# Attention and two mixture layers on one core: another start-up order, with mask rows of two pairs written in place and unread products

## The chip, the cores and the metric

The kernel runs on one core of a Trainium2 chip. The metric is the device time of one execution in microseconds; each version is run several times, and the median counts. The profile shows one execution, taken by the hardware profiler. The engines are named as in the profile: PE (TensorE, matrix products), PEld (its weight loads), DVE (VectorE), ACT (ScalarE), POOL (GpSimd), SP (SyncE, which issues all DMAs here).

## What is computed

A masked attention over 2 batches of 8 heads, then a soft mixture of experts, then a dense layer pair. All that the change touches is in the attention:

```python
def _attn_ref(q, k, v, proj):          # q, k, v: 2 x 8 x 768 x 64; proj: 64 x 6
    scale = 1.0 / np.sqrt(D)
    q_bits = (np.einsum('bhsd,dk->bhsk', q, proj) > 0).astype(np.int64)
    k_bits = (np.einsum('bhsd,dk->bhsk', k, proj) > 0).astype(np.int64)
    powers = 2 ** np.arange(n_bits)
    q_bucket = np.sum(q_bits * powers, axis=-1)
    k_bucket = np.sum(k_bits * powers, axis=-1)
    mask = q_bucket[:, :, :, None] == k_bucket[:, :, None, :]
    scores = scale * np.matmul(q, k.transpose(0, 1, 3, 2))
    scores = np.where(mask, scores, -1000000000.0)
    scores = scores - np.max(scores, axis=-1, keepdims=True)
    attn = np.exp(scores)
    attn = attn / (np.sum(attn, axis=-1, keepdims=True) + 1e-09)
    return np.matmul(attn, v).astype(np.float32)

x = _moe_ref(x=x, **moe_kwargs)        # x: 1536 x 512
return _moe2_ref(x=x, **moe2_kwargs)   # h = x @ w_in; (h - tanh(h)) @ w_out
```

## The kernel before

The 16 heads are worked in 8 pairs of two heads (0 to 7). For each pair, q and k come in by DMA (`load_qk`, tiles `tq`, `tk`), PE transposes them into PSUM (`t_unit`), ACT and DVE copy the result to `xq` and `xk` (128 rows: 64 of each head). The operands of the scores are the tiles `QA` and `KA` (per head 128 rows: rows 0 to 63 the rounded q or k, rows 64 to 87 the mask rows, row 96 the row of maxima) and `QB` and `KB` (rounded parts and what the rounding left over, written by `lo` and by the copies of `dups`). `his` writes the first 64 rows of `QA` and `KA`.

The mask rows come from the sign bits of q and k times `proj`. For pair 0, `bits0` makes two products of 24 rows and 768 columns on PE, DVE compares them with zero (`bt0`), and `rows0` scales the bits and writes them straight into rows 64 to 87 of `QA` or `KA`, on ACT, DVE or POOL. For all other pairs `bits` makes four products of 384 columns that stand in four column groups of PE, one comparison, one scaling (`rt`), and eight DMAs copy the rows from `rt` into `QA` and `KA`.

`m_unit` makes the scores of 128 queries (PE, `pm`, two products over 96 rows) and DVE takes their maxima (`mx`, one reduction for each of 12 blocks of a pair). `m_fin` transposes the maxima, and makes from them a row `row` for row 96 of `QA` and flags `zrow` of queries without a partner; both are copied by DMA, the flags four times into `z`. `v_unit` and `v_unit2` make a mean of v that those queries get. `s_unit` makes the scores `pst` from `KA`, `QA`, `KB`, `QB` (four products), ACT takes the exponential, POOL adds the results up (`es`), and `av_unit` multiplies with v into `pav`.

In PSUM one pool hands out three buffers in turn to all of `pt`, `pb`, `pm`, `pc`, `pv`, `pst` and to `cl` of the conversion of `w_in` (`win_load`, `win_cvt`: one ACT and three DVE instructions for each of 16 pieces `raw` of 512 KB). An instruction that needs a buffer waits for the last reader of what stood there three requests earlier.

Nothing here is ordered by a scheduler: the list `START` is worked off once, then `STEP` for each pair (`LAST` for the last). A word is a unit and the pair that it works on (in `STEP` the pair is the current one plus the unit's role). Each engine executes its own instructions in this order, and so does SP with its DMAs; a DMA is issued when what it waits for is done, and those behind it wait. At most eight DMAs are in flight: each waits for the one eight places ahead. `warm` in `START` makes PE products over zeros that nobody reads.

Of the kernel before, what the change touches and what calls it, by code (L numbers as in the profile page):

```python
# [1337 lines left out]
```

## Time and profile before

| | us |
|---|---|
| median of 3 runs | 494.92 (493.47 to 500.78) |
| the profiled execution's own time | 497.41 |
| its span, first to last instruction | 495.5 |
| PE busy | 467.0 (94%) |
| DVE, POOL, ACT busy | 332.7, 298.6, 271.7 |
| mean granted PE clock | 0.963 of 2.4 GHz |

The span is what the views of the trace divide up; 1.9 us of the execution's own time lie around it. Busy times are sums over stages that have different limits, so a stage is read for itself, from its waits and from what each engine did in it. In the granted clock, 1.00 is 2.4 GHz and 0.50 is 1.2 GHz.

### The profile page before, as it was taken

How to read it: one execution, taken by the hardware profiler on the slowest of the kernel's cores; microseconds unless marked ns; L12 is line 12 of the kernel's file. 1: busy time of each engine (PE TensorE's matmuls, PEld its weight loads, DVE VectorE, ACT ScalarE, POOL GpSimd, SP SyncE). 2: the span in 40 equal slices, each digit the busy share in tenths (PEclk: the TensorE clock that was granted, in tenths of full speed). 3: DMA queues.
4: the chain of work that ended last, by engine and by line, in shares of the span. 5: the costliest groups of instructions: out<-in, count | busy, mean ns of one | idle time of the engine just before them, and what ended most of it. 6: DMA issues, size and time to landing. Idle time of an engine off the chain costs nothing.

```text
span 495.5 us, 7422 instructions
## 1 busy us (share of the span) xinstructions
PE 467.0 (94%) x2634; PEld 302.5 (61%) x2634; DVE 332.7 (67%) x493; ACT 271.7 (55%) x463; POOL 298.6 (60%) x243
## 2 busy tenths in 40 slices
PE   7869999999999999999999899998999999999995
PEld 3445555556556565665565534557767677888884
DVE  5948687787887968648323564669999997544451
ACT  6252846638466384653444111167888887766671
POOL 4866976779687797867953120015677775444431
PEclk9559999999999999999999899997999999999998
DMA  6518157191650906829598899995000002100003
GB/s 211 130 29 234 56 127 190 40 232 48 162 151 20 248 15 160 279 55 333 167 340 337 298 366 385 352 408 235 1 1 0 2 0 86 43 1 1 1 1 133
DMA packets 51572, 72.83 MB, mean 147 GB/s; under 512 B 25604, under 2 KB 33480, under 8 KB 51528
## 3 DMA queue, kind: packets, MB, share of 16 engines
q1 hardware_dynamic: 51528, 72.28, 46.1%
q8 instruction: 23, 0.38, 0.3%
q14 instruction: 21, 0.17, 0.1%
HBM read 60.08 MB, written 3.15 MB: 128 GB/s over the span
## 4 chain that ended last, share of the span: by engine, by line
PE 60%; DVE 17%; DMA 7%; ACT 6%; SPq 4%; POOL 2%; issue 2%; DVEq 0%; ACTq 0%; POOLq 0%
PE pav L523 9%; PE po L1228 6%; PE po L1229 6%; PE po L1230 6%; PE pst L496 5%; PE pm L445 5%; PE pst L498 4%; DVE win L186 4%; DMA QB<-QA 3%; DVE mx L446 2%; SPq L150 2%; DVE win L1179 2%; PE pt L352 2%; PE po L913 2%; DVE win L191 2%
## 5 line engine op out<-in xcount | busy, mean ns | idle before, releaser
L511 POOL TENSOR_TENSOR es<-es,e 128x768 f32<-128x768 f32 x59 | 118.6, 2022 | 23.5 <-ACT e L500 22.8
L500 ACT ACTIVATE e<-pst 128x768 f32<-128x768 f32 x96 | 76.6, 807 | 92.2 <-PE pst L498 88.5
L446 DVE TENSOR_REDUCE mx<-pm 128x1 f32<-128x768 f32 x96 | 88.0, 952 | 20.8 <-PE pm L445 19.9
L523 PE MATMUL pav<-e,tv 128*64 128x256 f32 (+1 forms) x384 | 72.9, 498 | 0.0
L1209 POOL TENSOR_TENSOR split<-win,split 128x512 fp32r<-128x512 f32 x31 | 44.0, 1420 | 45.6 <-ACT split L1204 45.5
L445 PE MATMUL pm<-KA,QA 96*128 96x512 f32 x192 | 55.6, 391 | 5.2 <-DMA QA<-rt 3.1
L1209 POOL TENSOR_TENSOR ghl<-win,ghl 128x256 fp32r<-128x256 f32 x32 | 27.6, 862 | 49.8 <-ACT ghl L1204 49.8
L496 PE MATMUL pst<-QA,KA 128*128 128x512 f32 x192 | 56.2, 374 | 1.3 <-DVE bt L364 1.3
L1178 DVE SCALAR_TENSOR_TENSOR ph<-win,ph 128x512 f32<-128x512 f32 x64 | 35.7, 558 | 29.8 <-ACT win L1173 29.8
L1228 PE MATMUL po<-w,split 128*128 128x512 f32 x128 | 51.5, 402 | 0.0
L1229 PE MATMUL po<-w,split 128*128 128x512 f32 x128 | 51.4, 401 | 0.0
L1230 PE MATMUL po<-w,split 128*128 128x512 f32 x128 | 51.2, 400 | 0.0
L498 PE MATMUL pst<-QB,KB 128*128 128x512 f32 x192 | 50.6, 345 | 0.0
L523 PEld LDWEIGHTS pav<-e,tv 128*64 128x64 f32 x384 | 24.0, 136 | 39.3 <-issue 39.1
L445 PEld LDWEIGHTS pm<-KA,QA 96*128 96x128 f32 x192 | 30.9, 201 | 27.3 <-issue 11.4
L505 POOL TENSOR_TENSOR es<-e 128x768 f32<-128x768 f32 x16 | 29.3, 1831 | 24.7 <-PE pr L534 17.7
L1173 ACT ACTIVATE win<-ph 128x512 f32<-128x512 f32 (+1 forms) x64 | 30.8, 482 | 24.0 <-PE ph L1166 23.9
L1179 DVE SCALAR_TENSOR_TENSOR win<-win,ph 128x512 f32<-128x512 f32 x64 | 35.5, 555 | 8.6 <-ACT win L1173 0.5
L1174 ACT ACTIVATE win<-win,ct 128x512 f32<-128x512 f32 (+1 forms) x64 | 39.5, 617 | 2.1
L496 PEld LDWEIGHTS pst<-QA,KA 128*128 128x128 f32 x192 | 29.9, 194 | 16.0 <-issue 8.1
L498 PEld LDWEIGHTS pst<-QB,KB 128*128 128x128 f32 x192 | 30.3, 194 | 4.4
L1230 PEld LDWEIGHTS po<-w,split 128*128 128x128 f32 x128 | 24.6, 192 | 5.7
(243 smaller groups left out, 814.6 us busy)
## 6 DMA issues: line engine op xcount, KB each, us to landing
w<-in_moe_w_dram SPq DMA_DIRECT2D x32, 1024.0 KB
raw<-in_moe_w_in_dram SPq DMA_DIRECT2D x16, 512.0 KB
w<-in_moe_w_out_dram SPq DMA_DIRECT2D x8, 1024.0 KB
tv<-in_v_dram SPq DMA_DIRECT2D x8, 384.0 KB
out_dram<-win SPq DMA_DIRECT2D x12, 256.0 KB
tq<-in_q_dram SPq DMA_DIRECT2D x14, 192.0 KB
tk<-in_k_dram SPq DMA_DIRECT2D x14, 192.0 KB
QB<-QA SPq DMA_DIRECT2D x10, 192.0 KB
```

The lines of the kernel that those rows point to most:

```text
L445: nc.tensor.matmul(pm[:, c0:c1], QA[s][h][:96, c * P:(c + 1) * P], KA[s][h][:96, c0:c1], start=True, stop=True)
L446: nc.vector.reduce_max(mx[i][:, h * KT + c:h * KT + c + 1], pm, axis=AX.X)
L496: nc.tensor.matmul(pst[:, c0:c1], KA[s][h][:, c * P:(c + 1) * P], QA[s][h][:, c0:c1], start=True, stop=False)
L498: nc.tensor.matmul(pst[:, c0:c1], KB[t][h][:, c * P:(c + 1) * P], QB[t][h][:, c0:c1], start=False, stop=True)
L500: nc.scalar.activation(e, pst, AF.Exp, scale=0.125)
L511: eng.tensor_tensor(es[i, h][0], es[i, h][0], e, ALU.add)
L523: nc.tensor.matmul(pav[i][j][64 * h:64 * h + 64, :], tv[i][:, h, c, :], e2[h][:, c0:c1], start=False, stop=c == KT - 1, tile_position=(0, ...
L1179: nc.vector.scalar_tensor_tensor(g, w, Q_B, self.ph[p], ALU.add, ALU.mult)
L1209: (eng or nc.gpsimd).tensor_tensor(gl[p], g, gh[p].bitcast(F32), ALU.subtract)
L1228: nc.tensor.matmul(po, gh[p][:, us], wo.half(f, 0), start=f == 0, stop=False)
L1229: nc.tensor.matmul(po, gh[p][:, us], wo.half(f, 1), start=False, stop=False)
L1230: nc.tensor.matmul(po, gl[p][:, us], wo.half(f, 0), start=False, stop=f == NF - 1)
```

## The change

`START` is another list. In it:

- q and k of pair 0 are asked for first, then the constants `ct`, then two pieces `raw` of `w_in`, and then `blk` and the four small loads of `proj`. q and k of pair 1 come before `phi` and v; v of pair 1 is loaded in `START` too.
- All mask rows of pair 0 are written by POOL, those of a head ahead of its first maximum (before: those of head 0 after its last maximum, so that its maxima were taken without them).
- `bits0` and `rows0` now serve any pair, and pair 1's mask rows are made by them and written in place by ACT (`KA`) and POOL (`QA`), ahead of pair 1's maxima; its eight DMAs from `rt` go.
- POOL instead of ACT copies three blocks of 64 rows (`hp1.0`, `hp0.0`, `hp3.1`).
- The four copies of the flags leave `m_fin` for a unit of their own, `m_flag` (`fz`), which stands later in `START` and right behind `f2` in `STEP`.
- A new unit `keep` makes unread products of 32 rows and 128 columns from `ct`, 26 of them in `START`, the last ahead of the first scores; `warm` makes four products instead of three, over `phiB` (zeros at that time), into a buffer of the pool of `pav`.
- A unit that was done already is left out when `STEP` comes to it. From the first scores on, the instructions stand in the same order on every engine, except SP's loads of `w_in` and v, which were partly issued before.

```diff
-START = ("const.0 warm.3 qk.0 const.1 tq_aaaa.0 wl.0 oi.0 tk_aavv.0 h1.0 h0.0 bq.0 wl.0 bk.0 h2.0 "
+START = ("qk.0 warm.4 const.0 wl.0 oi.0 wl.0 const.1 tq_aaaa.0 tk_aavv.0 keep.2 bq.0 hp1.0 hp0.0 h3.0 bk.0 wq0p.0 keep.2 "
...
         nc.vector.memset(ones32, 1.0)
-        nc.vector.memset(phiB, 0.0)
...
-        def bits0(which):
-            x = (xqs, xks)[which][0]
+        def bits0(i, which):
+            x = (xqs, xks)[which][i]
...
-        def rows0(which, h, eng):
+        def rows0(i, which, h, eng):
...
-                y, b = X[0][h][rs, c0:c1], bt0[which][:, c0:c1]
+                y, b = X[i][h][rs, c0:c1], bt0[which][:, c0:c1]
...
-            for r in range(4):
-                if r % 2 in hs:
-                    j = r % 2 - hs[0]
-                    copy(zr[i][r:r + 1], zrow[KT * j:KT * j + KT, :])
+            zrows.setdefault(i, []).append((hs, zrow))
+
+
+        def m_flag(i):
+            for hs, zrow in zrows.pop(i):
+                for r in range(4):
+                    if r % 2 in hs:
+                        j = r % 2 - hs[0]
+                        copy(zr[i][r:r + 1], zrow[KT * j:KT * j + KT, :])
...
+        done = set()
+
         def unit(w, i):
+            if w in ("m", "s0", "s1", "a", "wl", "wc", "lp", "warm", "keep", "const"):
+                if w == "m" and nm.get(i) == 2 * KT - 1:
+                    return
+            elif (w, i) in done:
+                return
...
-            elif w == "warm":
+            elif w in ("warm", "keep"):
+
+                w_ = 256 if w == "warm" else P
                 for _ in range(i):
-                    nc.tensor.matmul(wt[:32, :256], wz[:, :32], wz, start=True, stop=True)
+                    nc.tensor.matmul(wt[0][:32, :w_], wz[:, :32] if w == "warm" else ident[:, :32], wz if w == "warm" else ident, start=True, stop=True)
...
-        wt, wz = psum("warm"), e_p.tile([P, 256], F32, tag="e", name="warm")
+        wt, wz = [pav_p.tile([P, 512], F32, tag="pav512", name="warm")], phiB.rearrange("p a b c -> p (a b c)")
```

On SP at the start of the program there stood before (`x4` is four instructions in a row):

```order
L153 DMA ct<-in_const_dram 128x298
L316 DMA tq<-in_q_dram 128x2x384
L316 DMA tk<-in_k_dram 128x2x384
L157 DMA blk<-in_const_dram 4x128
L161 DMA projb<-in_proj_dram 64x6 x4
L617 DMA raw<-in_moe_w_in_dram 128x1024 x2
L167 DMA phiB<-in_moe_phi_dram 64x4x32 x2
L326 DMA tv<-in_v_dram 128x2x384
```

and there stands now, up to the same load of v:

```order
L316 DMA tq<-in_q_dram 128x2x384
L316 DMA tk<-in_k_dram 128x2x384
L154 DMA ct<-in_const_dram 128x298
L622 DMA raw<-in_moe_w_in_dram 128x1024 x2
L158 DMA blk<-in_const_dram 4x128
L162 DMA projb<-in_proj_dram 64x6 x4
L320 DMA tq<-in_q_dram 128x6x64 x2
L320 DMA tk<-in_k_dram 128x6x64 x2
L167 DMA phiB<-in_moe_phi_dram 64x4x32 x2
L151 DMA kh_264<-KA_131 64x768
L326 DMA tv<-in_v_dram 128x2x384
```

The constants moved behind q and k, two pieces of `w_in` moved from behind the four small loads of `proj` to ahead of them, and pair 1's q and k moved ahead of v.

On POOL, from the first clearing of `KA` on, there stood before:

```order
L295 MEMSET KA_131 64x1536
L299 MEMSET KA_131 1x1536
L395 ISA
L395 TENSOR_SCALAR QA_127<-bt_194,ct 24x768
L428 TENSOR_TENSOR KB_138<-xk,KA_131 64x768
L395 TENSOR_SCALAR QA_127<-bt_194,ct 24x768
L432 TENSOR_TENSOR KB_138<-xk,kh_254 64x768
```

and there stands now (`KA_131` and `QA_127` are the operands of pair 0; the row `ISA` carries no operands, and the trace has no record of it):

```order
L295 MEMSET KA_131 64x1536
L299 MEMSET KA_131 1x1536
L403 CAST QA_127<-xq 64x768
L403 CAST KA_131<-xk 64x768
L395 ISA
L395 TENSOR_SCALAR QA_127<-bt_195,ct 24x768
L395 TENSOR_SCALAR KA_131<-bt_204,ct 24x768
L428 TENSOR_TENSOR KB_138<-xk,KA_131 64x768
L395 TENSOR_SCALAR KA_131<-bt_204,ct 24x768
L395 TENSOR_SCALAR QA_127<-bt_195,ct 24x768
L432 TENSOR_TENSOR KB_138<-xk,kh_264 64x768
```

Two copies moved ahead of the row `ISA`, and two writings of mask rows were added.

On PE, between the transposed maxima of pair 0 (`pc`) and the first scores (`pst`), there stood before:

```order
L452 MATMUL pc<-ct,mx 12x128
L352 MATMUL pt<-ct,tk 128x128 x6
L361 MATMUL pb<-xq,projb 32x384 x2
L361 MATMUL pb<-xk,projb 32x384 x2
L481 MATMUL pv<-va,ones_62 4x128
L496 MATMUL pst<-QA_127,KA_131 128x512
```

and there stands now (the rows `warm<-ct` are the products of `keep`):

```order
L452 MATMUL pc<-ct,mx 12x128
L700 MATMUL warm<-ct 32x128 x2
L382 MATMUL pb<-xk,projb 32x512
L382 MATMUL pb<-xk,projb 32x256
L700 MATMUL warm<-ct 32x128
L382 MATMUL pb<-xq,projb 32x512
L382 MATMUL pb<-xq,projb 32x256
L700 MATMUL warm<-ct 32x128 x2
L486 MATMUL pv<-va,ones_62 4x128
L700 MATMUL warm<-ct 32x128 x6
L501 MATMUL pst<-QA_127,KA_131 128x512
```

The transposes of pair 1's k moved ahead of `pc`, the bits of pair 1 became two products of full length for k and then q, and 11 unread products stand between. On DVE the same stretch read before:

```order
L446 TENSOR_REDUCE mx<-pm 128x1 x12
L177 TENSOR_SCALAR cl<-raw 128x512
L186 SCALAR_TENSOR_TENSOR cl<-cg,cl 128x512
L191 SCALAR_TENSOR_TENSOR win<-raw,cl 128x512
L395 TENSOR_SCALAR KA_131<-bt_202,ct 24x256
L455 TENSOR_SCALAR zrow<-pc 12x128
L456 SCALAR_TENSOR_TENSOR row<-zrow,pc 12x128
L364 TENSOR_SCALAR bt<-pb 128x384
L485 TENSOR_TENSOR vt<-pv,blk 4x128
```

and reads now, from the end of the twelve maxima:

```order
L455 TENSOR_SCALAR zrow<-pc 12x128
L456 SCALAR_TENSOR_TENSOR row<-zrow,pc 12x128
L177 TENSOR_SCALAR cl<-raw 128x512
L186 SCALAR_TENSOR_TENSOR cl<-cg,cl 128x512
L191 SCALAR_TENSOR_TENSOR win<-raw,cl 128x512
L384 TENSOR_SCALAR bt_339<-pb 24x512
L384 TENSOR_SCALAR bt_339<-pb 24x256
L384 TENSOR_SCALAR bt_354<-pb 24x512
L384 TENSOR_SCALAR bt_354<-pb 24x256
L177 TENSOR_SCALAR cl<-raw 128x512
L186 SCALAR_TENSOR_TENSOR cl<-cg,cl 128x512
L191 SCALAR_TENSOR_TENSOR win<-raw,cl 128x512
```

The row of maxima moved ahead of the first conversion, four comparisons replace one, and the second conversion, which stood behind `vt`, now stands ahead of it. `vt` follows in both, and then pair 1's remainder `QB` and its maxima.

## Rows read from the trace of the kernel before

**Rows 1.** Windows of the run: busy us (instructions) of each engine, granted clock, DMA share, GB/s:

```profile
12.00:15.00 3.00, 2.15 (x7) 1.22 (x8) 3.00 (x4) 1.58 (x3) 1.19 (x2) 0.97 0.95 210
15.00:20.00 5.00, 4.95 (x12) 2.59 (x11) 5.00 (x7) 0.10 (x1) 4.85 (x4) 0.50 0.89 211
...
28.00:34.00 6.00, 2.90 (x9) 2.13 (x10) 2.76 (x4) 3.47 (x6) 5.03 (x5) 0.50 0.21 46
34.00:40.00 6.00, 5.54 (x19) 4.47 (x19) 3.67 (x4) 1.62 (x2) 2.35 (x3) 0.61 0.33 76
40.00:46.00 6.00, 5.95 (x32) 3.44 (x32) 5.39 (x7) 1.29 (x2) 3.88 (x2) 1.00 0.98 276
46.00:60.00 14.00, 13.11 (x80) 7.06 (x75) 9.87 (x16) 10.38 (x16) 12.34 (x10) 1.00 0.40 110
60.00:100.00 40.00, 38.16 (x216) 22.99 (x215) 30.65 (x41) 23.47 (x34) 28.62 (x20) 1.00 0.48 117
100.00:150.00 50.00, 49.58 (x285) 29.34 (x283) 41.67 (x55) 29.03 (x42) 40.87 (x29) 1.00 0.54 142
```

**Rows 2.** Chain of work that ended last, first 60 us: start, us, what:

```profile
1.19 3.22 DMA tq<-in_q_dram
...
7.14 2.78 PE pb L382 x8
...
9.95 1.03 DVE bt L384 x2
...
31.72 1.96 DMA QA<-rt
...
40.83 8.95 DMA tv<-in_v_dram
```

**Rows 3.** Timeline, PE: start, us, line, tiles, records; idle before and its releaser:

```profile
1.18 2.77 PE L679 MATMUL warm<-warm 128*32 128x256 f32 x6 [1.18 <-DVE projb L154]
...
5.81 0.88 PE L341 MATMUL pt<-ct,tk 128*128 128x128 f32 x6 [0.41 <-DMA tk<-in_k_dram]
...
33.82 0.98 PE L445 MATMUL pm<-KA,QA 96*128 96x512 f32 x2 [3.10 <-DMA QA<-rt]
...
35.88 1.48 PE L445 MATMUL pm<-KA,QA 96*128 96x512 f32 x4
...
39.54 0.97 PE L445 MATMUL pm<-KA,QA 96*128 96x512 f32 x4 [0.46 <-ACT e L500]
```

**Rows 4.** Timeline, the other engines, same columns:

```profile
5.17 1.07 SPq L617 DMA_DIRECT2D raw<-in_moe_w_in_dram  x2
...
8.66 1.02 DVE L384 TENSOR_SCALAR bt<-pb 24x512 f32<-24x512 f32 x2 [0.81 <-PE pb L382]
...
9.80 0.98 POOL L395 TENSOR_SCALAR QA<-bt,ct 24x768 fp32r<-24x768 f32 x1 [6.28 <-DVE bt L384]
...
10.86 1.81 POOL L428 TENSOR_TENSOR KB<-xk,KA 64x768 fp32r<-64x768 f32 x1
...
11.01 10.47 DVE L446 TENSOR_REDUCE mx<-pm 128x1 f32<-128x768 f32 x12
...
14.48 0.97 POOL L395 TENSOR_SCALAR QA<-bt,ct 24x768 fp32r<-24x768 f32 x1 [1.81 <-PE pm L445]
...
21.39 0.68 DVE L177 TENSOR_SCALAR cl<-raw 128x512 uint32<-128x512 uint32 x1
...
22.91 0.69 DVE L191 SCALAR_TENSOR_TENSOR win<-raw,cl 128x512 uint32<-128x512 uint32 x1
...
26.28 1.41 POOL L299 MEMSET KA<- 1x768 f32 x2
...
34.84 0.96 DVE L446 TENSOR_REDUCE mx<-pm 128x1 f32<-128x768 f32 x1 [3.29 <-PE pm L445]
...
39.11 2.91 DVE L446 TENSOR_REDUCE mx<-pm 128x1 f32<-128x768 f32 x3 [0.53 <-PE pm L445]
```

**Rows 5.** Windows of 1 us while the two pieces of `w_in` came in:

```profile
8.00:9.00 1.00, 1.00 (x5) 0.44 (x4) 0.34 (x1) 1.00 (x3) 0.00 (x0) 1.00 1.00 397
9.00:10.00 1.00, 1.00 (x5) 0.27 (x3) 0.73 (x3) 0.97 (x2) 0.20 (x1) 1.00 1.06 327
```

More of the change, by code (lines that the diff above doesn't have):

```diff
@@ L60 @@
 RING, HOLD = (4, 2, 2, 4, 3, 1, 3, 1), 4
-START = ("const.0 warm.3 qk.0 const.1 tq_aaaa.0 wl.0 oi.0 tk_aavv.0 h1.0 h0.0 bq.0 wl.0 bk.0 h2.0 "
-        "h3.0 wq1p.0 m.0 m.0 m.0 l0.0 m.0 const.2 m.0 v.0 wk1a.0 m.0 m.0 m.0 wq0p.0 m.0 kc.0 m.0 "
-        "m.0 qk.1 l2.0 m.0 wl.0 d.0 wc.0 wk0s.0 t0.1 f2.0 h1.1 t1.1 l1.0 h3.1 l3.0 v1.0 h2.1 "
-        "kc.1 oi.1 b.1 v2.0 wc.0 wc.0 h0.1 qk.2 oi.2 wl.0").split()
+START = ("qk.0 warm.4 const.0 wl.0 oi.0 wl.0 const.1 tq_aaaa.0 tk_aavv.0 keep.2 bq.0 hp1.0 hp0.0 h3.0 bk.0 wq0p.0 keep.2 "
[3 rows of a table added]
+        "oi.2 qk.2 keep.2 keep.2 kc.1").split()
 STEP = ("s0 a s1 l1 m s0 m xr xe m s1 wl v m m m s0 lp l0 m lp a m m s1 l2 e00 a m m d a wc wl e01 v1 s0 s1 t1 h0 lp l3 "
-        "wl s0 t0 m lp h3 a e02 lp v2 lp f2 h1 x2 s1 e03 b x3 wl wc s0 a h2 s1 qk lp lg kc lp wc").split()
+        "wl s0 t0 m lp h3 a e02 lp v2 lp f2 fz h1 x2 s1 e03 b x3 wl wc s0 a h2 s1 qk lp lg kc lp wc").split()
 LAST = ("s0 lp lp a s0 xe lp s1 s0 xr lp a s1 x2 x3 lg a lp s1 s0 s0 s0 lp s1 a s1 a s1 lp a lp").split()
@@ L405, in his @@
                 nc.scalar.activation(X[s][h][:64], x[i][r0], AF.Copy)
-        kh1 = {}
+        kh1, zrows = {}, {}
         def kh1_copy(i):
@@ L421, in dups, with lo @@
                 copy(KB2[t][:64], KA2[s][:64])
-        def lo(i, w):
+        def lo(i, w, eng=None):
             s, t = i % 3, i % 2
-            eng = nc.gpsimd if i < 1 else nc.vector
+            eng = eng or (nc.gpsimd if i < 1 else nc.vector)
             if w == 0:
@@ L452, in m_fin @@
             nc.tensor.transpose(m, mx[i][:, hs[0] * KT:(hs[-1] + 1) * KT], ident)
-            zrow, row = (pre.tile([n * KT, P], F32R, tag=t, name=t) for t in ("zrow", "row"))
+            zrow, row = (pre.tile([2 * KT, P], F32R, tag=t, name=t)[:n * KT] for t in ("zrow", "row"))
             nc.vector.tensor_scalar(zrow, m, -0.5 * MASK, None, ALU.is_lt)
@@ L671, in s_next @@
                 [x for x in queue if x[1] == c and x[0] == i][0][2][1] = e
+        done = set()
         def unit(w, i):
+            if w in ("m", "s0", "s1", "a", "wl", "wc", "lp", "warm", "keep", "const"):
[3 more added lines that the diff above has]
+                return
+            else:
+                done.update({(w, i), (w.replace("hv", "h").replace("hp", "h").replace("lv", "l"), i)})
+            if w == "f2" and (("fa", i) in done):
+                if ("fb", i) not in done:
+                    unit("fb", i)
+                return
             if w in ("wl", "wc"):
@@ L707, in attention @@
             unit(u, int(n))
+        del wt[:]
         for i in range(NPR):
```

7 lines of the change are left out of this document (4 added, 3 removed), and 3 rows, old and new, of the table START.

## The prediction

> **What bounds the kernel now.** I read the windows of the run first. From 46 us on PE is busy 13.11 of 14, then 38.16 of 40, then 49.58 of 50 us [rows 1]. Behind that point both versions have the same instructions in the same order, so PE works off a fixed list there, and what the start gains or loses arrives at the end nearly one for one. So only the first 42 us count, until the sixth maximum of pair 1 (end at 39.11 + 2.91 = 42.02 [rows 4]).
>
> That stretch is a chain of waits, not an engine at its limit. The chain of work that ended last shows it [rows 2]: q lands at 4.41, the bits of pair 0 take PE 2.78, a comparison 1.03, then DVE makes twelve maxima in 10.47 us (0.87 each) [rows 4], and later PE waits 3.10 us for the last mask row of pair 1 to arrive by DMA, until 33.82 [rows 3]. In parallel the granted clock falls from 1.00 to 0.50 just before 15 us, while PE made one block of products per maximum and waited for DVE in between, and it stays at 0.50 until some time in 34 to 40 [rows 1]. The products of two maxima took 1.48 us at 1.2 GHz and 0.97 at 2.4 GHz [rows 3].
>
> **The change part by part.** The sum is made in the profiled execution (span 495.5, own time 497.41); the median 494.92 lies 2.5 below that, and I carry the difference over to the median.
>
> *Order of the first loads.* PE's first transposes need `tq` and `ct`, both of which had landed by 4.41 [rows 2]. Now `ct` is the third load. The same three loads stood first before, and the third (`tk`) was seen at 5.81 [rows 3]. So the transposes start between 4.54 and 5.81; I take 5.4, since the bytes ahead are the same and the first q is issued one place earlier: +0.9 us. ACT's copies of q move with them, to 8.0 instead of 7.1.
>
> *Two pieces of `w_in` ahead of `proj`.* The bits need `proj`. Before, its four small loads were issued ahead of the pieces (those at 5.17 [rows 4]) and had landed when PE started the bits at 7.14 [rows 2]. Now 1 MB stands ahead of them. At the 362 GB/s of the two windows in which such pieces came in [rows 5] that is 2.9 us behind `ct`, so `proj` lands near 5.4 + 2.9 = 8.3. Bounds: 8.0, if small loads pass the large ones (then ACT's copies decide), and 10.4, at the 211 GB/s of 15 to 20 [rows 1]. I take 8.3: bits 1.2 us late. That loads of one issuer are worked off in order is seen at v of pair 1, whose 384 KB took 8.95 us behind q, k and two pieces [rows 2].
>
> The Trainium skill says the same ("DMA: Bandwidth & Descriptors", Queues, rings and completion order: on each DMA engine descriptors are consumed in ring order), and this speaks against the change here; the 8.95 us agree with it. Without the rule the bits would start 0.3 us earlier.
>
> *Mask rows ahead of the maxima.* From the start of the bits to the first maximum it took 3.87 us (7.14 to 11.01 [rows 2, 4]): two products and the comparisons, with PE's first block of scores hidden under the last comparison. Now the first block waits until POOL has written `KA`'s rows behind that comparison: 0.98 like the row at 9.80, 0.12 to hand over as there [rows 4], then about 0.6 for the products and their hand-over to DVE (0.49 a block at 2.4 GHz [rows 3]). First maximum: 8.3 + 3.87 + 1.1 + 0.6 = 13.9, so 2.9 us late. The copies of head 0 that POOL now makes ahead of it cost between 0.98 (a one-input row of 24 partitions) and 1.81 (two inputs, 64 partitions) [rows 4]; I take 1.0, the one-input row. They wait for q and k only and end near 10, while bits are still compared; they cost nothing unless POOL is held up (the second case below).
>
> *Twelve maxima* keep DVE's pace: 13.9 + 10.5 = 24.4 instead of 21.48. Seven unread products stand between the last six blocks. A product of 256 columns took 2.77 / 3 = 0.92 us at the start [rows 3], so 128 columns cost 0.46 then, and 0.23 at twice that pace (the bits, 1536 columns in 2.78 us [rows 2]). At 1.2 GHz six blocks and seven products need 6 x 0.74 + 7 x 0.46 = 7.7 us of PE against 5.2 of DVE; three buffers let PE run ahead by some 1.7, so up to 0.8 us may show. At 2.4 GHz, 4.5 us, nothing.
>
> *From the last maximum to pair 1's first.* Before: 21.48 to 34.84, 13.4 us, the end of it set by rows from `rt` by DMA. Those DMAs go. What is late next is DVE: PE's first block of pair 1 needs the buffer that `vt` reads, and ahead of `vt` stand the row of maxima (0.6 and 0.5 to wait for `pc`), a conversion (21.39 to 23.60, 2.2 [rows 4]), two comparisons of full length (1.03 each), a second conversion (2.2) and `vt` (0.3): 7.9 us. Scores of pair 0 wait behind the same comparisons. POOL is as late: it worked without a pause from 14.48 to 27.69 [rows 4]; this list of 13.2 us now starts at about 16.2 (`KA`'s first row at 13.2, then 1.9 and 1.0), ends at 29.4, and a copy and two mask rows of pair 1 follow: 32.4. So the block starts near 32.3 to 32.9 and the maximum at 33.4, if the bits of pair 1 run at 2.4 GHz. At 1.2 GHz they need 5.6 instead of 2.8 us and transposes and `pc` some 1.4 more; then DVE waits for PE, and the block comes near 36.9.
>
> *The clock.* The 26 unread products fill waits. Between maxima 1 and 6 there are none, and there PE did fall to 0.50 before [rows 1]; I expect it to fall again. From maximum 7 on, at 1.2 GHz, PE has no more time to wait than shown above, and the one place where the clock rose in this stretch was after 34, where PE was busy 5.54 of 6 us [rows 1]. So I expect it back near 25, ahead of pair 1's bits, instead of in 34 to 40. Six maxima of pair 1 then take about 6.3 us (six reductions of 0.96 and a little waiting) instead of 7.2: 0.9 gained.
>
> *The rest.* Flags in a unit of their own change no order in `STEP`; in `START` they leave SP later, and their first reader, the first `av` of pair 0, stands behind several scores and maxima. v of pair 1, for which POOL waited to 49.8 [rows 2], comes early: at most 1 us off POOL, and no more. `done` only shapes the list.
>
> Sum: pair 1's first maximum at 33.4 instead of 34.84 (-1.4) and six faster ones (-0.9 to -1.0): **-2.4 us, 492.5 us**.
>
> **The rivals.** *POOL is held up behind its copies.* Between clearing `KA` and the first mask rows POOL's list has the row `ISA`, of which the trace shows no record. Before, it stood in a pause of 6.28 us [rows 4], which can hide anything up to that length; that the pause ended 0.12 us after the comparison of q's bits (8.66 + 1.02 = 9.68) speaks for less. Now it stands behind the two copies, which end at about 10.1. If it takes R, mask rows come at 10.1 + R, 0.98 and 0.98 more, against 13.2 needed; it costs from R = 1.1 on, and at R = 6.2 the first maximum comes 5.1 us later than in my sum, with everything behind it: 492.5 + 5.1 = **497.6 us, slower than before**. The Trainium skill has a rule for such a hold ("GPSIMD Engine Reference", Instruction dispatch: the first call of a freshly loaded kernel costs about 6 us more, without a visible row). By that figure, an estimate, the time would be about 497.4; the pause of before neither shows nor excludes it.
>
> *The clock stays low.* If the products do not bring it back before pair 1's bits, the block comes at 36.9, 3.1 us later than before, and the six maxima gain nothing: **498 us**. For it speaks that 4.95 of 5 us of modelled PE time at 15 to 20 did not raise it [rows 1]; against it, that PE still waited for each of those maxima and will not now.
>
> *The clock never falls and `proj` is not late.* Then pair 1's first maximum comes at about 31.5 and the sum is -4 to -5: **490 us**. Against it stand maxima 1 to 6 without any filling.
>
> **How the numbers follow.** My forecast, 490.5 to 494.5, has 0.54; POOL held up 0.25 (496 to 498.5, with R from 4 to 6.3); the clock low 0.13; the full gain 0.08. From the upper two cases I reach to 499, where a long hold and a low clock together (500) are left out, and to 489.5 below: the range is 489.5 to 499. What a measurement of this kernel can tell from no change is about 2%, 10 us. No case reaches that alone: faster by more would need a quarter of the first 42 us (0.03, the runs' own spread included); slower by more needs the hold, the low clock and `proj` at 10.4 together, 5.1 + 5.5 + 2.1 (0.04). Within 2%: 0.93.
>
> **What would show it.** In the profile of the changed kernel: the transposes near 5.4, the bits near 8.3, the first maximum near 13.9 (wrong if before 12 or after 16), POOL's first mask row at the comparison's end (held up if it starts 4 us or more behind its copies with the comparison long done), a granted clock of 0.50 from about 15 to 25, no DMA wait ahead of pair 1's first block, that block near 32.6, and the sixth maximum's end near 39.6. A forecast of gain is wrong if that end lies at 42 or later, or if PE's share behind 46 us falls.

## The result and the profile after

| | before | after |
|---|---|---|
| median (20 runs each) | 495.38 (493.47 to 505.38) | 501.23 (496.23 to 507.87) |
| ratio after/before, 95% interval | | 1.0101 (1.0078 to 1.0125) |
| the profiled execution's own time, span | 497.41, 495.5 | 504.15, 502.4 |
| mean granted clock | 0.963 | 0.973 |

The change costs about 1%, 5 us, where 2.4 us of gain were forecast. The ratio leaves disturbed executions out; the profiled one of after is among its longer ones, so its rows show where time went and the runs how much.

Windows of the run of after, as [rows 1] (busy us and instructions of PE, PEld, DVE, ACT and POOL, granted clock, DMA share, GB/s):

```profile
5.00:10.00 5.00, 1.64 (x8) 1.67 (x9) 0.00 (x0) 0.72 (x2) 0.00 (x0) 0.75 0.59 210
10.00:12.00 2.00, 2.00 (x10) 1.18 (x9) 0.74 (x2) 1.93 (x5) 0.82 (x1) 0.50 0.32 74
...
15.00:20.00 5.00, 2.51 (x20) 1.83 (x17) 2.95 (x6) 0.00 (x0) 3.76 (x3) 1.00 0.97 244
20.00:25.00 5.00, 4.50 (x14) 2.44 (x13) 4.56 (x6) 0.00 (x0) 4.88 (x4) 0.62 0.17 42
25.00:28.00 3.00, 3.00 (x11) 1.95 (x11) 2.68 (x4) 0.00 (x0) 2.85 (x3) 0.50 0.00 0
28.00:34.00 6.00, 5.67 (x31) 4.21 (x29) 3.18 (x6) 2.10 (x4) 5.72 (x9) 0.71 0.01 3
34.00:40.00 6.00, 4.79 (x30) 2.83 (x28) 5.50 (x11) 5.11 (x7) 2.76 (x4) 1.00 0.23 51
...
100.00:150.00 50.00, 49.58 (x282) 30.00 (x280) 42.86 (x54) 27.47 (x40) 37.78 (x27) 1.00 0.59 152
```

PE did 1.64 us of work between 5 and 10. The clock is at 0.50 by 10 to 12, back at 1.00 for 15 to 20, and low again between 20 and 34; from 34 on it is 1.00, where before it rose only in 34 to 40 [rows 1]. From 100 to 150 PE is as full as before. Chain of work that ended last, as [rows 2]:

```profile
4.95 3.35 DMA projb<-in_proj_dram
8.36 2.85 PE pt L341 x12
11.21 0.99 PE warm L700 x4
12.20 2.56 PE pb L382 x5
15.95 1.04 DVE bt L384 x2
17.09 0.98 POOL KA L395
18.11 0.63 PE pm L445 x2
18.76 2.70 DVE mx L446 x3
21.50 1.01 PE pm L445 x2
22.51 0.99 PE warm L700 x4
...
27.22 1.85 PE warm L700 x8
```

This names the loss of the start: loads until 8.36, bits at half speed, POOL's row of `KA`, and then the unread products (`warm L700`) themselves, which stand on the chain among the maxima. The two products ahead of the bits (11.21) cost nothing: the last of the `proj` loads was complete only at 11.61, as the section on the loads shows. Timeline of PE and of the other engines, as [rows 3, 4] (`xN` counts records; a product has two):

```profile
8.36 1.51 PE L341 MATMUL pt<-ct,tq 128*128 128x128 f32 x6 [3.83 <-DMA projb<-in_proj_dram]
...
12.00 2.62 PE L382 MATMUL pb<-xq,projb 128*32 128x512 f32 x4
...
18.11 1.32 PE L445 MATMUL pm<-KA,QA 96*128 96x512 f32 x6 [2.15 <-POOL KA L395]
```

```profile
15.80 0.97 POOL L395 TENSOR_SCALAR QA<-bt,ct 24x768 fp32r<-24x768 f32 x1 [2.65 <-DVE bt L384]
17.09 0.97 POOL L395 TENSOR_SCALAR KA<-bt,ct 24x768 fp32r<-24x768 f32 x1 [0.31 <-DVE bt L384]
...
18.76 5.28 DVE L446 TENSOR_REDUCE mx<-pm 128x1 f32<-128x768 f32 x6 [1.78 <-PE pm L445]
24.47 1.82 DVE L446 TENSOR_REDUCE mx<-pm 128x1 f32<-128x768 f32 x2 [0.44 <-PE pm L445]
26.62 1.82 DVE L446 TENSOR_REDUCE mx<-pm 128x1 f32<-128x768 f32 x2 [0.32 <-PE pm L445]
30.05 1.82 DVE L446 TENSOR_REDUCE mx<-pm 128x1 f32<-128x768 f32 x2 [1.60 <-PE pm L445]
...
41.48 0.96 DVE L446 TENSOR_REDUCE mx<-pm 128x1 f32<-128x768 f32 x1 [0.36 <-PE pm L445]
42.73 4.57 DVE L446 TENSOR_REDUCE mx<-pm 128x1 f32<-128x768 f32 x5 [0.28 <-PE pm L445]
```

The transposes start at 8.36 instead of 4.54, the bits at 12.00 instead of 7.14, the first maximum at 18.76 instead of 11.01. The twelve maxima run from 18.76 to 31.87, 13.1 us instead of 10.47, with DVE waiting for PE three times. From there to pair 1's first maximum it takes 9.6 us instead of 13.4, without a DMA. Pair 1's sixth maximum ends at 42.73 + 4.57 = 47.30, before at 42.02: **5.3 us late**. At the middle of the attention (the 37th exponential) 4.2 are left. Further back stands another loss, at 246. Timeline there, DVE, then PE:

```profile
242.16 2.31 DVE L435 TENSOR_TENSOR QB<-xq,QB 64x768 fp32r<-64x768 f32 x1 [3.87 <-DMA QB<-QA]
244.39 0.94 DVE L446 TENSOR_REDUCE mx<-pm 128x1 f32<-128x768 f32 x1
```

```profile
245.48 0.27 PE L452 MATMUL pc<-ct,mx 128*12 128x128 f32 x1 [2.82 <-DVE mx L446]
```

In the kernel before, the same wait is 1.07 us and the writing of `QB` 1.08 (DVE, then PE):

```profile
237.43 1.08 DVE L435 TENSOR_TENSOR QB<-xq,QB 64x768 fp32r<-64x768 f32 x1 [3.34 <-DMA QB<-QA]
239.53 0.27 PE L452 MATMUL pc<-ct,mx 128*12 128x128 f32 x1 [1.07 <-DVE mx L446]
```

Behind the longer wait the granted clock is at 0.57 for 246 to 250, and the exponentials, 4.2 us later than before up to there, are 7.5 later from then on. Window of after:

```profile
246.00:250.00 4.00, 4.00 (x17) 3.08 (x17) 1.61 (x5) 1.30 (x2) 2.97 (x4) 0.57 0.64 254
```

### The profile page after: what moved, and what is told of

Same layout as the page of the kernel before. It is cut to its first block, busy times and chain, and to the rows that moved or that the text cites. A ratio compares the mean times of both kernels' runs of the same rounds, so it can differ in the third digit from the quotient of the medians.

```text
span 502.4 us, 7519 instructions
## 1 busy us (share of the span) xinstructions
PE 471.3 (94%) x2688; PEld 305.8 (61%) x2688; DVE 336.1 (67%) x494; ACT 268.3 (53%) x459; POOL 304.8 (61%) x250
## 4 chain that ended last, share of the span: by engine, by line
PE 65%; DVE 19%; ACT 5%; DMA 4%; SPq 3%; issue 2%; DVEq 0%; POOL 0%; ACTq 0%
PE pav L528 12%; PE pm L445 7%; PE pst L501 7%; PE pst L503 5%; PE po L1251 5%; PE po L1250 5%; PE po L1252 5%; DVE win L186 4%; DVE win L1201 3%; DMA QB<-QA 3%; PE po L935 2%; DVE win L191 2%; PE pt L352 2%; PE pl L598 2%; SPq L151 2%
## 5 line engine op out<-in xcount | busy, mean ns | idle before, releaser
L445 PE MATMUL pm<-KA,QA 96*128 96x512 f32 x192 | 54.4, 384 | 3.5 <-POOL KA L395 2.1
L1250 PE MATMUL po<-w,split 128*128 128x512 f32 x128 | 50.5, 394 | 0.0
L1251 PE MATMUL po<-w,split 128*128 128x512 f32 x128 | 50.4, 394 | 0.0
L1252 PE MATMUL po<-w,split 128*128 128x512 f32 x128 | 50.3, 393 | 0.0
L528 PEld LDWEIGHTS pav<-e,tv 128*64 128x64 f32 x384 | 24.1, 136 | 39.6 <-issue 39.4
L1195 ACT ACTIVATE win<-ph 128x512 f32<-128x512 f32 (+1 forms) x64 | 30.7, 480 | 21.6 <-PE ph L1188 21.6
```

The lines of the kernel that those rows point to most:

```text
L445: nc.tensor.matmul(pm[:, c0:c1], QA[s][h][:96, c * P:(c + 1) * P], KA[s][h][:96, c0:c1], start=True, stop=True)
L528: nc.tensor.matmul(pav[i][j][64 * h:64 * h + 64, :], tv[i][:, h, c, :], e2[h][:, c0:c1], start=False, stop=c == KT - 1, tile_position=(0, ...
L1250: nc.tensor.matmul(po, gh[p][:, us], wo.half(f, 0), start=f == 0, stop=False)
L1251: nc.tensor.matmul(po, gh[p][:, us], wo.half(f, 1), start=False, stop=False)
L1252: nc.tensor.matmul(po, gl[p][:, us], wo.half(f, 0), start=False, stop=f == NF - 1)
```

## The experiments

In the edits, words of `START` have a pair behind the dot; `wl` loads a piece of `w_in`, `const.0` is `ct`, `const.1` is `blk` and `proj`. Four markers, in us: start of pair 0's first maximum (M1), duration of the twelve (M1 to the end of the last), start of pair 1's first maximum (P1) and of its sixth (P6). They come from one trace of each kernel, the ratios from several runs. Two traces of the start of after (after and after_max_first, the same instructions up to there) differ by 1.2 to 1.5 us in them.

| kernel | ratio to before (95%) | M1 | twelve | P1 | P6 |
|---|---|---|---|---|---|
| before | 1 | 11.01 | 10.5 | 34.84 | 41.07 |
| after | 1.0101 (1.0078 to 1.0125) | 18.76 | 13.1 | 41.48 | 46.34 |
| win_behind_proj | 1.0055 (1.0019 to 1.0091) | 15.17 | 13.1 | 37.81 | 42.64 |
| const_first | 1.0016 (0.9971 to 1.0062) | 13.72 | 13.1 | 36.42 | 41.26 |
| no_keep | 1.0139 (1.0100 to 1.0179) | 18.47 | 10.5 | 41.39 | 47.47 |
| before_win_ahead | 1.0160 (1.0105 to 1.0216) | 16.77 | 10.5 | 40.97 | 47.59 |
| quiet_maxima | 0.9978 (0.9940 to 1.0017) | 13.33 | 10.5 | 33.87 | 38.72 |
| late_rows | **0.9899 (0.9868 to 0.9931)** | 11.57 | 10.5 | 32.42 | 37.28 |
| late_rows_no_keep | 0.9929 (0.9886 to 0.9972) | 11.57 | 10.5 | 33.36 | 38.43 |
| old_list | 1.0008 (0.9961 to 1.0055) | 12.52 | 10.5 | 36.30 | 42.53 |
| late_rows_loads | 1.0041 (1.0005 to 1.0078) | 15.81 | 10.5 | 36.60 | 41.42 |
| late_rows_full_keep | 0.9908 (0.9876 to 0.9941) | 11.57 | 12.5 | 34.95 | 39.80 |
| late_rows_one_cvt | 0.9952 (0.9911 to 0.9993) | 11.29 | 10.5 | 32.07 | 36.74 |
| late_rows_short | 0.9972 (0.9937 to 1.0007) | 11.57 | 10.5 | 33.20 | 37.85 |
| after_max_first | 1.0042 (1.0011 to 1.0074) | 17.54 | 13.1 | 40.04 | 44.87 |
| late_rows_max_first | 0.9898 (0.9854 to 0.9942) | 11.57 | 10.5 | 32.36 | 37.19 |
| late_rows_ct_third | 0.9942 (0.9907 to 0.9977) | 12.09 | 10.5 | 32.91 | 37.76 |
| late_rows_win_ahead | 0.9995 (0.9960 to 1.0029) | 15.07 | 10.5 | 35.88 | 40.74 |

**The loads.** Three kernels first, two from after and one from before.

```diff
@@ win_behind_proj, from after @@
-qk.0 warm.4 const.0 wl.0 oi.0 wl.0 const.1 tq_aaaa.0
+qk.0 warm.4 const.0 oi.0 const.1 wl.0 wl.0 tq_aaaa.0
@@ const_first, from after @@
-qk.0 warm.4 const.0 wl.0 oi.0 wl.0 const.1 tq_aaaa.0
+const.0 warm.4 qk.0 const.1 wl.0 oi.0 wl.0 tq_aaaa.0
@@ before_win_ahead, from before @@
-const.0 warm.3 qk.0 const.1 tq_aaaa.0 wl.0 oi.0
+const.0 warm.3 qk.0 wl.0 wl.0 const.1 tq_aaaa.0 oi.0
```

> The changed kernel, with the two loads of w_in moved behind the four small loads of proj and nothing else. Theory 1 (the loads): the w_in pieces, not the copies or the mask rows, made the start late; transposes then begin near 5.2 instead of 8.36, pair 0's bits near 7.8 instead of 12.0, the first maximum near 13.5 instead of 18.8, and the time falls by 4 to 5 us against the changed kernel, to within 1 us of the kernel before or below it. Theory 2 (the products and the rows ahead of the maxima): the late loads are mostly hidden, PE falls to 1.2 GHz in any case; the first maximum still comes after 16 and the time stays within 1.5 us of the changed kernel, near 500.

> The changed kernel with the old order of the first loads: ct, q, k, blk, proj, then the two pieces of w_in. Theory 1: as with w_in behind proj, and the transposes begin where they did before, at 4.5, bits at 7.1 to 7.3, the first maximum at 12.7; the time is 0 to 1 us below the run with w_in behind proj. Theory 2: no difference of over 1 us from the changed kernel.

> The kernel before with one thing changed: the two loads of w_in moved ahead of the four small loads of proj. Theory 1: the bits of pair 0 start at 10 to 12 instead of 7.14, and the kernel is 3 to 5 us slower than before. Theory 2: less than 1 us slower. A third possibility, that the pieces also hold up the loads issued ahead of them: then the first transposes, which wait for ct and q alone, begin later than 4.54 here too; if only the loads behind are held up, they begin at 4.5.

`w_in` behind `proj` brings M1 3.6 us forward, `ct` first as well 5.0 (2.4 and 3.8 against after_max_first). M1 still comes 1.7 and 1.0 us later than expected. The same two pieces put ahead in the kernel before cost it 5.8 us at M1 and 6.5 at P6. So the loads are a loss in either list. Timeline of before_win_ahead, PE:

```profile
4.39 1.30 PE L340 MATMUL pt<-ct,tq 128*128 128x128 f32 x6 [0.45 <-DMA tq<-in_q_dram]
6.88 0.84 PE L340 MATMUL pt<-ct,tk 128*128 128x128 f32 x6 [1.19 <-DMA tk<-in_k_dram]
10.38 2.74 PE L381 MATMUL pb<-xq,projb 128*32 128x512 f32 x4 [2.66 <-DMA projb<-in_proj_dram]
12.91 2.77 PE L381 MATMUL pb<-xk,projb 128*32 128x512 f32 x4
```

`proj` is waited for until 10.38, and behind that wait both bits run at half speed, 5.3 us (to 15.68) instead of 2.78. The first transposes are not late here (4.39), but those of k, whose load stands right ahead of the pieces in this list, start at 6.88 instead of 5.81. Even so const_first is no faster than before: other losses remain.

**The unread products.** no_keep is after without any `keep`; quiet_maxima is const_first without the seven products between the first and the last `m.0`.

```diff
@@ no_keep, from after, and so on through the list @@
-tk_aavv.0 keep.2 bq.0 hp1.0 hp0.0 h3.0 bk.0 wq0p.0 keep.2 h2.0 wk0p.0 keep.3 l0.0 wk1p.0 keep.1 qk.1
+tk_aavv.0 bq.0 hp1.0 hp0.0 h3.0 bk.0 wq0p.0 h2.0 wk0p.0 l0.0 wk1p.0 qk.1
...
@@ quiet_maxima, from const_first @@
-m.0 m.0 m.0 m.0 keep.1 keep.1 m.0 m.0 kc.0 v.0 keep.1 m.0 m.0 keep.2 keep.1 keep.1 m.0 m.0
+m.0 m.0 m.0 m.0 m.0 m.0 kc.0 v.0 m.0 m.0 m.0 m.0
```

> The changed kernel without any of the 26 unread products of keep (warm stays). Theory 1: transposes still begin near 8.4 and bits near 11; the first maximum near 17.7; the maxima of pair 0 take 10.5 us instead of 13.1, but the clock returns later (after 38), so that the sixth maximum of pair 1 comes at 46 to 48 and the time is within 1.5 us of the changed kernel. Theory 2: the products themselves cost the start 3 us or more, and the time falls to 497 or less.

> The list of const_first without the seven unread products that stood between the twelve maxima of pair 0 (the other 19 stay). If PE at 1.2 GHz was the pace there, the maxima take 10.5 us again instead of 13.1 (13.7 to 24.2) and pair 1's first maximum comes 2.0 to 2.6 us earlier than in const_first (36.4), near 34; ratio 0.996 to 0.999. Rival: the seven products bring the clock back, so without them PE stays at 1.2 GHz through pair 1's bits; then the first maximum of pair 1 stays at 36 to 37 and the six maxima behind it take over 5.5 us; ratio 1.002 or more.

Without the seven, the maxima take 10.5 us again and P6 comes 2.5 us earlier (38.72 against 41.26); the intervals of the two ratios overlap, so this rests on the markers. Taking out all 26 costs at P6 more than it gives: no_keep has the fast maxima and still the latest P6 of the kernels made from after (47.47), with the clock at 0.50 from 18.1 to 35.2 and 38.6 to 45.4, although its transposes began 1.2 us earlier (7.15). By the ratios no_keep and after are not told apart (1.0139 and 1.0101, the intervals overlap). The products help behind the maxima and hurt among them.

**Mask rows of pair 0 back behind its maxima.** late_rows takes loads, rows and maxima in the order of before, and from the last maximum on the changed list:

```diff
-qk.0 warm.4 const.0 wl.0 oi.0 wl.0 const.1 tq_aaaa.0 tk_aavv.0 keep.2 bq.0 hp1.0 hp0.0 h3.0 bk.0 wq0p.0
...
-m.0 m.0 t1.1 l2.0 d.0 t0.1 f2.0 keep.2 wc.0
+const.0 warm.4 qk.0 const.1 tq_aaaa.0 wl.0 oi.0 tk_aavv.0 h1.0 h0.0 bq.0 wl.0 bk.0 h2.0 h3.0 wq1p.0 qk.1
+m.0 m.0 m.0 l0.0 m.0 const.2 m.0 wk1a.0 m.0 m.0 m.0 wq0p.0 m.0 kc.0 v.0 m.0 m.0 m.0
+t1.1 l2.0 wk0s.0 d.0 t0.1 f2.0 keep.2 wc.0
...
```

Behind that it is after's list, with its 11 products. late_rows_no_keep drops these 11; old_list is the changed program with the list of before.

> Loads, pair 0's mask rows and its maxima in the order of the kernel before; from the last maximum of pair 0 on the changed list, with its mask rows of pair 1 in place and its 11 unread products there; no unread products ahead. If the in-place rows of pair 1 are the gain and all the rest the loss, the first maximum of pair 0 comes at 11, its last ends at 21.5, pair 1's first maximum comes 9 to 10 us later, at 31 to 32 instead of 34.8, and everything behind is 3 to 5 us earlier; ratio 0.990 to 0.994. Rival: with no unread products ahead the clock stays at 0.50 to 35 or later, pair 1's bits and scores run at half speed, and the first maximum comes at 34 to 36; ratio 0.998 to 1.003.

> late_rows without any unread product behind warm. If the 11 products behind the maxima raise the clock, this one has it at 0.50 until about 38 as in the kernel before, pair 1's first maximum 1.5 to 3 us later than in late_rows and six maxima that take over 6 us from first to last start; ratio 0.996 to 1.0. If they do nothing, both give the same times within 0.5 us up to pair 1's sixth maximum.

> The changed program with the list START of the kernel before (three warm products, eight DMAs from rt for pair 1, no unread products, the flags' copies right behind the row of maxima), STEP as changed. If START alone carries the loss, it is the kernel before: pair 1's first maximum at 34.8 within 0.5, ratio 0.998 to 1.002. If the flags' unit or the skipped repeats cost something, the time is over 1.003 and the stretch behind 46 us is longer.

late_rows is 1.0% **faster** than before and the first of these that clearly beats both kernels. Timelines of late_rows, DVE, and of late_rows_no_keep, DVE:

```profile
11.57 10.46 DVE L445 TENSOR_REDUCE mx<-pm 128x1 f32<-128x768 f32 x12
...
32.42 0.96 DVE L445 TENSOR_REDUCE mx<-pm 128x1 f32<-128x768 f32 x1 [0.19 <-PE pm L444]
33.65 4.57 DVE L445 TENSOR_REDUCE mx<-pm 128x1 f32<-128x768 f32 x5 [0.27 <-PE pm L444]
```

```profile
33.36 0.96 DVE L445 TENSOR_REDUCE mx<-pm 128x1 f32<-128x768 f32 x1 [1.13 <-PE pm L444]
```

Against quiet_maxima, M1 is 1.8 and P6 1.4 us earlier: that is the price of rows ahead of the maxima, less what their writing costs later. (The eight unread products ahead of the maxima and POOL's two copies go with the rows; they were not tried alone.) Pair 1's rows in place, with the rest of the changed order behind the maxima, bring 4.1 us at P6 (38.43 against old_list's 42.53, whose start was 1.0 late by slow bits) or 2.6 against before; the 11 products add 1.15, less at P1 (0.9) than expected. The half-speed stretch that begins near 14 ends at 24 in both, but without them the clock falls once more, at 30.7 for 3.4 us. old_list is the kernel before within its interval: `START` carries the loss, not the flags' unit.

**The loads once more, alone.** Three variants of late_rows, in which only the first words differ (where `wl.0` stands twice, the one behind `bq.0` is left out):

```diff
-const.0 warm.4 qk.0 const.1 tq_aaaa.0 wl.0 oi.0
@@ late_rows_loads @@
+qk.0 warm.4 const.0 wl.0 oi.0 wl.0 const.1 tq_aaaa.0
@@ late_rows_ct_third @@
+qk.0 warm.4 const.0 const.1 tq_aaaa.0 wl.0 oi.0
@@ late_rows_win_ahead @@
+const.0 warm.4 qk.0 wl.0 oi.0 wl.0 const.1 tq_aaaa.0
```

> late_rows with the first loads in the changed order: q and k, then ct, then two pieces of w_in, then blk and proj. If the loads are the main loss, the transposes start at 7 to 8.4 instead of 4.7, the bits of pair 0 at 11 to 12 instead of 7.7, and all that follows comes 4 to 5 us later than in late_rows: pair 1's first maximum at 36.5 to 37.5, ratio 0.998 to 1.001. Rival: the wait at the start moves the clock's fall and rise too (as where w_in went ahead in the kernel before, +8); then over 6 us later, ratio over 1.003. If the loads cost only the 1.2 us of the forecast, ratio 0.991 to 0.994.

> late_rows with q and k ahead of ct, and w_in behind proj as there. If ct's place alone costs what the forecast said, the transposes start at 5.4 to 5.8 instead of 4.7, the bits at 8.2 to 8.6, pair 0's first maximum at 12.0 to 12.6, ratio 0.990 to 0.993. Rival: ct comes late by itself as in the changed kernel, transposes at 7 or later, ratio 0.996 or more.

> late_rows with ct first and two pieces of w_in ahead of blk and proj. If proj waits behind the pieces, the transposes stay at 4.7, the bits start at 10 to 10.6, the first maximum comes at 14 to 14.6, ratio 0.995 to 0.999. The 8.3 of the forecast would give bits at 8.3 to 8.6 and a ratio of 0.990 to 0.992.

Timelines of PE: late_rows_ct_third, then late_rows_loads, then late_rows_win_ahead.

```profile
5.63 0.85 PE L340 MATMUL pt<-ct,tq 128*128 128x128 f32 x6 [0.83 <-DMA ct<-in_const_dram]
...
8.22 1.48 PE L381 MATMUL pb<-xq,projb 128*32 128x512 f32 x4 [0.46 <-ACT xq L347]
```

```profile
8.12 1.51 PE L340 MATMUL pt<-ct,tq 128*128 128x128 f32 x6 [3.33 <-DMA ct<-in_const_dram]
...
11.51 1.92 PE L381 MATMUL pb<-xq,projb 128*32 128x512 f32 x4 [0.54 <-DMA projb<-in_proj_dram]
```

```profile
4.73 1.54 PE L340 MATMUL pt<-ct,tq 128*128 128x128 f32 x6
...
9.54 2.18 PE L381 MATMUL pb<-xq,projb 128*32 128x512 f32 x4 [2.28 <-ACT QA L404]
11.51 2.46 PE L381 MATMUL pb<-xk,projb 128*32 128x512 f32 x4
```

`ct` as third load, with nothing large behind it, costs 0.9 us at the transposes and 0.5 at M1. With two pieces of `w_in` issued **behind** it, it is 8.12 before PE has it, 2.5 us later still. `w_in` ahead of `proj` alone costs 1.8 us at the start of the bits and, with the bits slower behind the wait, 3.5 at M1. Both together: 4.2 at M1, and 0.0142 of the time (1.0041 less 0.9899), 7 us. 4.1 of that stand at P6; the rest comes behind 236 us, where this kernel shows a half-speed stretch of 6.8 us from 241.

The traces also hold sixteen landing events for each of these loads, and PE starts behind the last one. In after those of `ct` came from 4.75 to 6.28, but the last at 8.23, 0.13 ahead of the transposes. The events of the last `proj` load had 9.16 as their middle one and 11.61 as their last, 0.39 ahead of the bits at 12.00. In late_rows_win_ahead the last came at 9.15, again 0.39 ahead of the bits, so there too they waited for `proj`; the profile names ACT's writing of `QA`, which the bits do not read. In late_rows_ct_third all sixteen of `ct` lie between 4.92 and 5.49. So most of a load is in early, and PE waits for a late last part. How late differs: a third load with 1 MB queued right behind it was complete 1.1 to 2.7 us later than without in five traces (`ct` at 7.02 to 8.23 against 5.49, `tk` at 6.74 in before_win_ahead against 5.67 in before) and 0.1 later in a sixth (`tk` at 5.89 in late_rows_win_ahead, 5.78 in late_rows).

**Filling from the first maximum.** late_rows with two products behind every block of pair 0's maxima:

```diff
-m.0 m.0 m.0 l0.0 m.0
+m.0 keep.2 m.0 keep.2 m.0 keep.2 l0.0 m.0 keep.2
...
```

> late_rows with two unread products behind each block of scores of pair 0's maxima, from the first on. If filling from the first maximum keeps the clock at 1.00, the twelve maxima take 10.5 us and transposes, row of maxima and bits behind them run at full speed: pair 1's first maximum 0.5 to 1.5 us earlier than in late_rows (32.4), ratio 0.986 to 0.990. If the clock falls all the same, a block and two products take PE 1.6 us at 1.2 GHz against DVE's 0.87: the maxima take 15 to 19 us, pair 1's first maximum comes at 37 to 41, ratio 1.0 to 1.007.

The result lies between the two cases. The clock stays at 1.00 from 6 to 487 us, and still the maxima take 12.5 us: a block and two products take PE 1.10 us (they start at 10.40, 11.50, 12.60 and so on), more than DVE's 0.87. Transposes and bits behind them are faster, but from the last maximum to P1 it takes 10.8 us as against 10.4 in late_rows, so P1 is 2.5 late. By the ratios the two kernels are only 0.5 us apart, but each interval reaches 1.5 us to either side, and the spans of the two traces differ by 1.7 us (490.1 and 488.4): whether the 2.5 us are won back later is not shown. Windows of late_rows_full_keep:

```profile
10.00:15.00 5.00, 5.00 (x28) 2.81 (x26) 4.60 (x7) 2.71 (x4) 2.78 (x2) 1.00 1.09 253
15.00:20.00 5.00, 5.00 (x29) 2.96 (x29) 4.28 (x6) 0.00 (x0) 3.29 (x3) 1.00 0.68 166
20.00:25.00 5.00, 5.00 (x34) 3.35 (x31) 4.09 (x5) 0.40 (x1) 4.69 (x5) 1.00 0.00 0
```

**A shorter list on DVE.** late_rows_one_cvt drops the second conversion ahead of `vt` (that piece is converted later; of the two words taken out, the one behind `v.1` found nothing to convert); late_rows_short besides makes head 0's row of `KA` on ACT and puts `f2.0` ahead of `t0.1`.

```diff
@@ both @@
-wc.0 v.1 wc.0 keep.2
+v.1 keep.2
@@ late_rows_short @@
-t1.1 l2.0 wk0s.0 d.0 t0.1 f2.0
+t1.1 l2.0 wk0a.0 d.0 f2.0 t0.1
```

> late_rows without the second conversion of w_in ahead of vt (the piece is converted later in the program). If DVE's list between last maximum and vt is what pair 1's first maximum waits for, that comes 1.5 to 2.2 us earlier (30.2 to 30.9 instead of 32.4), and the end 1 to 2 us earlier; ratio 0.986 to 0.989. Rival: PE's own list, POOL's mask rows or ACT end as late; then at most 0.5 us earlier, and the conversion that is made later eats it; ratio 0.989 to 0.992.

> late_rows_one_cvt with two more edits: head 0's row of KA made by ACT alone instead of ACT and DVE, and the maxima of pair 0 transposed ahead of pair 1's q. DVE's list is another 1.2 us shorter and its wait for pc goes; the first conversion starts 1 us earlier. If DVE stays the pace, pair 1's first maximum comes at 29 to 30; ratio 0.983 to 0.987. Rival: the bits of pair 1 come no earlier (their transposes at 1.2 GHz end at the same time), so that it ties with late_rows_one_cvt within 0.5 us.

Both fell short: in the first P1 came 0.35 earlier (M1 was already 0.28 earlier), and in the second 0.8 later. In both DVE was done early and waited 2.5 us for PE's scores; PE in turn waited 1.61 us for POOL's mask rows. Timeline of late_rows_short, PE:

```profile
32.55 0.61 PE L444 MATMUL pm<-KA,QA 96*128 96x512 f32 x2 [1.61 <-POOL QA L394]
```

Their ratios are worse than their P6 suggests; both show the half-speed stretch near 237.

**The loss at 246.** In the seventh pass of `STEP` the last maximum of the last pair goes ahead of the writing of `QB`:

```diff
-lp l3 wl s0 t0 m lp
+lp wl s0 t0 m l3 lp
```

> The changed kernel with one swap in the seventh pass of STEP: the last maximum of the last pair stands ahead of DVE's writing of QB, which took 2.31 us there beside POOL's sums (1.08 in the kernel before). If that slow writing is what made PE wait 2.82 us for pc and let the clock fall at 246, the wait is under 1 us, there is no half-speed stretch there, the offset to the kernel before stays at +4 to +4.5 past that point, and the ratio falls from 1.010 to 1.003 to 1.006. Rival: the late loss has nothing to do with it (the clock falls there or soon after anyway, or PE waits for QB instead); ratio 1.008 or more.

> The same swap in late_rows, which had no half-speed stretch there and a wait of 1.12 us. If the wait is all it costs there, 0.5 to 1.1 us faster than late_rows: ratio 0.986 to 0.990. If PE then waits for QB instead, as late_rows, 0.988 to 0.992.

Timeline of after_max_first, DVE, then PE:

```profile
239.77 0.96 DVE L446 TENSOR_REDUCE mx<-pm 128x1 f32<-128x768 f32 x1 [2.64 <-PE pm L445]
240.65 0.95 DVE L435 TENSOR_TENSOR QB<-xq,QB 64x768 fp32r<-64x768 f32 x1
```

```profile
241.42 0.28 PE L452 MATMUL pc<-ct,mx 128*12 128x128 f32 x1
```

The wait is gone, no half-speed stretch follows, and the ratio falls from 1.0101 to 1.0042: 2.9 us of the loss were there (the intervals, 1.0011 to 1.0074 and 1.0078 to 1.0125, just part). The swap takes two things out of the maximum's way, the slow writing and its wait for a DMA (3.87 us in after, 3.34 in before), and does not tell them apart. The slow writing alone does not make the wait: in late_rows_no_keep it took 2.61 us, and PE waited 1.06. In late_rows, whose wait was short, the swap gives nothing; PE then waited 1.65 us for `vt`, behind a writing of `QB` that took 1.97.

## Why the prediction was wrong

- *Order of the first loads*, and *Two pieces of `w_in` ahead of `proj`*: these steps failed. The first priced `ct` by the loads ahead of it alone (5.4). As third load it does come then (5.63), but not with 1 MB behind it (8.36 in after, 8.12 in late_rows_loads). The second put `proj` at the bytes' end, 8.3, with 10.4 as its outer bound. The middle landing event of the last `proj` load, 9.16, is not far from that; its last was at 11.61, and the bits began at 12.00. "Worked off in order" was taken to mean that a load lands when its own bytes are through, but PE waits for its last part, and in after that came 3.1 us (`ct`) and 2.4 us (the last `proj` load) behind the middle one. The same section of the Trainium skill that was quoted for the order ("DMA: Bandwidth & Descriptors", Queues, rings and completion order) says besides that completion is not first in, first out for one issuing engine. The trace of after agrees: the first landing event of a piece of `w_in` came at 6.40, ahead of the last of `ct`, issued earlier, at 8.23. Why the last part is late is not settled.
- What the wait does to the clock was left out altogether. In after PE waited 3.83 us ahead of the transposes, the clock fell to 0.50 at 7.5, and transposes and bits ran at 1.2 GHz (2.62 us for one of the two bits, 1.48 in late_rows); both bits took 3.9 us instead of 2.78. Waits of 2.28 in late_rows_win_ahead and 2.66 in before_win_ahead also went with slow bits.
- *Mask rows ahead of the maxima*: forecast 1.1 + 0.6 us, measured 1.8 (quiet_maxima against late_rows) and 2.2 (const_first, with the same list up to there). Right, or slightly low.
- *Twelve maxima*: forecast at most 0.8 us over DVE's pace, measured 2.6. The PE time of the step was right in kind (seven products and six blocks at 1.2 GHz exceed DVE); the credit of 1.7 us for running ahead was not. The clock fell at 21.2, during the first six maxima, and DVE's three waits (0.44, 0.32, 1.60) pay nearly the whole excess.
- *From the last maximum to pair 1's first*: forecast 9.0 us, measured 9.6. Right, and so was its reason: no DMA is waited for, and `vt` at 39.99 stands behind the two conversions, as the step said. Six maxima took 5.8 us (41.48 to 47.30) instead of 7.2, more than the 0.9 forecast.
- *The clock*: forecast 0.50 from 15 to 25 and back before pair 1's bits; it was low from 7.5 to 14 and from 21 to 31, and back before those bits (33.44). The first of the two falls was not in the forecast; the second came 6 us late and lasted as long as forecast.
- The rivals: POOL was not held up. In const_first its second copy ended at 9.55 and the first mask row began at 10.37, 0.82 later and 0.11 behind the end of the comparison (10.26), so the row `ISA` cost no more than 0.82 there. The full gain did not come, and the clock was not low in the place that the rival named.
- *What bounds the kernel now*: that only the first 42 us count and that a loss there arrives nearly one for one did not hold. No step saw the 2.9 us at 246: DVE's writing of `QB` took 2.31 us there, PE waited longer, and the clock fell. That the shifted start made the writing slow is not shown: with late_rows' start it took 0.95 us, and 1.97 after the swap.

Sum at pair 1's sixth maximum, by the pairs of kernels: rows in place 2.6 and the products behind the maxima 1.2 to the good; loads 4.1, products among the maxima 2.5 and rows ahead 1.4 to the bad: 4.2 us late, between the 3.8 of after_max_first (44.87 less 41.07) and the 5.3 of after. (The loads' term is from the variants of late_rows, the others from other lists; that they add up is not shown otherwise.) Against the forecast, after is late by 3.7 us at the start of the bits, 4.9 at the first maximum, 7.5 at the end of the twelve and 7.7 at the end of pair 1's sixth (47.30 against 39.6).

## What to carry to other kernels

Keep large loads behind every load that the first instructions need, and not only in the order of issue: one queued right behind a needed load can delay it too, by 1.1 to 2.7 us in five of six traces here. Put unread products where PE has time to spare, and not between products that another engine is waiting for: here 11 behind the maxima gave 1.2 us and 7 among them cost 2.5. A change in a start-up list moves the phase of everything behind it, so look for waits that grew far from the edit.
